# Four x tiles on one DMA queue, the key weights behind ScalarE's table load, and a first stage reordered to match

## The chip, the cores and the metric

The kernel runs on one core of a Trainium2 chip. The metric is the device time of one execution in microseconds (us), the median of several runs of the same program. The core has a matrix engine (TensorE, "PE" in the profile, with its weight loads shown as "PEld"), VectorE ("DVE"), ScalarE ("ACT"), GpSimd ("POOL") and SyncE ("SP"). Each engine runs its own instructions in order; engines meet through semaphores. Loads and stores are issued by an engine into that engine's DMA queue and are carried out by 16 DMA engines that all queues share. In this kernel SP, ACT and POOL issue DMAs.

## The reference

The input `x` has 2048 rows of 512. The block is a linear attention with 32 heads of 16, followed by a gated MLP that mixes the rows; both have a layer norm in front and a residual around them.

```python
# A: linear attention on layernorm(x)
q, k, v = split(x_norm @ wqkv)               # 32 heads of 16
phi = lambda t: where(t > 0, t + 1, exp(t)) + 1e-6
pq, pk = phi(q), phi(k)
kv = einsum('bhsd,bhse->bhde', pk, v)
z  = einsum('bhsd->bhd', pk)
o  = einsum('bhqd,bhde->bhqe', pq, kv) / (einsum('bhqd,bhd->bhq', pq, z) + 1e-6)
h  = x + o @ wo
# B: gated MLP with spatial mixing on layernorm(h)
z1, z2 = split(gelu(h_norm @ w_in)); z2 = layernorm(z2)
g   = einsum('ts,bsf->btf', w_sp, z2) + b_sp
out = h + (z1 * g) @ w_out
```

## The kernel before

The 2048 rows are 16 tiles of 128 rows, called tile 0 to tile 15. The first stage, about the first 41 us, does this for each tile:

- a DMA brings the tile (128 KB) from `A_x`; tiles 0 to 3 come one by one, later ones in pairs, and the last four in one DMA;
- VectorE takes its statistics (`stats`, L576, then `aggr`, L580);
- the reciprocal root is made on ScalarE (L590, L592) for tiles 0 to 3 and on GpSimd (L595, L597) for pairs of later tiles;
- VectorE normalises it (`normalise`, L611);
- it is transposed: tiles 0 to 3 by four TensorE transposes (L645, called T0 to T3 here) and a ScalarE copy out of PSUM (L652); tiles 4 to 15 by a DMA transpose that SP issues (L637);
- TensorE multiplies it with the key weights (`kv_proj`, L734, four matmuls of 128x128x512, called K0 to K15), which need the transposed tile and the weights `wk`;
- ScalarE and VectorE make phi of a pair of tiles (L711, L713, L714, L717, L720);
- TensorE accumulates the product of phi(k) and the normalised x (L766, in units of two matmuls, called X here).

Query projections (`q_proj`, L748, units of four matmuls, called Q) need four transposed tiles and the weights `wq`; they are filled in between. Sums over phi(k) (L782) close the stage. After that come the denominators, the attention output (L904), the two halves of the MLP's first matmul (L936, L967), the row mixing (L1006) and the output projection (L1024).

TensorE also runs matmuls on constants (`keep_busy`, L564): eight when the kernel starts, two after the first statistics, one of 512 columns after the first reciprocal root, and two pairs of 256 columns that are placed behind T0 and T1 in the order written out by hand. They change no result.

The order of every engine is not decided while the kernel is built. `ORDER` lists all operations by number, and each engine issues its own operations in that sequence; `SLOT` gives, for each tile of PSUM and of the scratch buffers in turn, the buffer that it takes. `Program.schedule` turns both into per-engine lists, and `_waits` into semaphore waits: an operation waits for what its data and its buffer need, and everything behind it on its engine waits with it. The costs written beside the operations take no part in what the chip does.

Before the change the first DMAs are issued so: SP issues x tile 0, x tile 2, x tile 3, `wq`, then the x tiles 4-5, 6-7, 8-9, 10-11 and 12-15; ScalarE issues x tile 1 and `wk`, and then loads its function table (L555). GpSimd fills constants: the identity for the transposes (L526, L527), `eps` (L530), masks (L538 to L542) and a selection matrix (L548, L550).

Of the kernel before, what the change touches and what calls it, by code (L numbers as in the profile page):

```python
# [12 lines left out]


ORDER = [
# [34 lines left out]
]  # L50
SLOT = [
# [104 lines left out]
class Program:  # L156
# [14 lines left out]
    def op(self, eng, cost, fn, r=(), w=(), bias=0.0, after=(), dma=None, nbytes=0, land=2.0, lag=None,  # L171
           mode=0):
        o = Op()
        o.eng, o.fn, o.cost, o.seq = eng, fn, cost, len(self.ops)
        o.bias, o.land, lag = bias + self.bias, land, self.LAG[eng] if lag is None else lag
        o.late, o.start, o.mode = self.late, None, mode
        o.after, o.deps, o.tiles = list(after) + self.first_of.get(eng, []), {}, []
        o.marked, o.sem, o.semval, o.grp, o.bytes, o.lag = False, None, None, dma, nbytes, lag
        o.raw = set()
        for x in list(r) + list(w):  # L180
            t = getattr(x, "tile", None)
            if t is not None and t not in o.tiles:
                o.tiles.append(t)
                t.ops.append(o)
        rk = [k for x in r for k in x.keys]
        wk = [k for x in w for k in x.keys]
        for k in rk:
            p = self.writer.get(k)
            if p is not None:
                o.deps[p] = True  # L190
                o.raw.add(p)
        for k in wk:
            p = self.writer.get(k)
            if p is not None:
                o.deps[p] = True
            for q in self.readers.get(k, ()):
                if q is not o:
                    o.deps[q] = True
        for k in rk:
            self.readers.setdefault(k, []).append(o)  # L200
        for k in wk:
            self.writer[k] = o
            self.readers[k] = []
        self.ops.append(o)
        return o
# [149 lines left out]
def bass_sequential_preLN__linear_attn_block__mixer_gmlp__prompt_kernel(  # L355
# [11 lines left out]
    _, S, D = A_x.shape  # L367
# [41 lines left out]
    wqkv = View(s_w3, 0, [KD, 3 * D], BF16)  # L409
# [84 lines left out]
    def load(eng, name, dst, src, nbytes, bias=0.0, behind=(), cost=0.5):  # L494
        o = op(eng, cost, lambda e: e.dma_start(dst.ap(), src), w=[dst], dma=(name, False), nbytes=nbytes,
               bias=bias, land=2.3)
        for p in behind:
            o.deps[p] = True
        return o

    w3 = A_wqkv.rearrange("(c p) f -> p c f", p=P)
# [3 lines left out]
    def load_x(eng, a, b, bias=BIG, **kw):  # L505
        more = {2: 40e3, 3: 60e3, 4: 70e3}.get(a, 0)
        xl[a] = load(eng, f"x{a}", x[a:b, :], x_dram[a * P:b * P, :].rearrange("(n p) d -> p n d", p=P),
                     int((b - a) * P * D * 2 + more), bias, **kw)

    load_x("sp", 0, 1)  # L510
    load_x("act", 1, 2)
    load("act", "wk", wqkv[:, D:2 * D], w3[:, :, D:2 * D], D * D * 2)
    load_x("sp", 2, 3)
    load_x("sp", 3, 4)
    load("sp", "wq", wqkv[:, 0:D], w3[:, :, 0:D], D * D * 2)
# [20 lines left out]
    def blocks(t, n, w, size):  # L536
# [18 lines left out]
    table = op("act", 1.3, lambda e: e.preload_act_table_set("natural_log_exp_and_others"), bias=BIG - 1,  # L555
               after=[o for o in g.ops if o.eng == "act"])
    g.first_of["act"] = [table]

    idle = Tile(PS)
    warm = []  # L560
# [523 lines left out]
```

## Time and profile before

| what | value |
|---|---|
| median of 3 runs | 241.23 us (240.99 to 241.85) |
| profiled execution, its own time | 241.31 us |
| span of that execution, first to last instruction | 240.1 us |
| granted TensorE clock, mean over the span | 1.000 |
| TensorE busy | 235.3 us |
| VectorE, ScalarE, GpSimd busy | 132.8, 78.6, 33.3 us |

The profiled execution takes 1.2 us more than its span: that part lies before the first and after the last instruction. A busy time counts an engine's instructions from start to end. The profile has several views: the page with its totals; the chain of waits that ended last, in order of time; the timeline of instructions; the DMA issues with their time from issue to landing; and a table of busy times by stretches. In the timeline a row has the start, the duration, the engine, the line, what is written and read, how many instructions were merged (`x4`), and in brackets the idle time before it and what ended it. `SPq` and `ACTq` rows are DMA issues: their duration is the issuing engine's time, not the transfer's. The chain counts an operation from the end of the one before it, so its starts can differ from the timeline's by up to 0.2 us.

### The profile page before, as it was taken

The page shows a single profiled execution, that of the slowest core. Times are in us where ns is not written, and L with a number is a line of the kernel's source. Part 1 is how long each engine was busy: PE and PEld are TensorE (multiplying, and loading weights), DVE is VectorE, ACT ScalarE, POOL GpSimd, SP SyncE. Part 2 cuts the span into 40 slices and gives each one's busy share as a digit, 9 for nine tenths or more (in the row PEclk, how much of TensorE's full clock was granted, in tenths as well). Part 3 has the DMA queues.
Part 4 walks back from the last instruction along what each step waited for, and adds up shares of the span by engine and source line. Part 5 has one row for each costly group of instructions (what it writes and reads, how often), then busy time and mean ns, then how long its engine had stood idle before and what let it go on. Part 6 is the DMA issues. An engine that isn't in the chain of part 4 may idle for free.

```text
span 240.1 us, 3026 instructions
## 1 busy us (share of the span) xinstructions
PE 235.3 (98%) x1172; PEld 110.2 (46%) x1194; DVE 132.8 (55%) x269; ACT 78.6 (33%) x101; POOL 33.3 (14%) x84
## 2 busy tenths in 40 slices
PE   7999999999999999999999999999999999999996
PEld 2544444554444444444444444444444444444443
DVE  4898884489999882938533233351332523323444
ACT  3783843884487698665400000000000000000000
POOL 7131303000334514235000000000000000000000
DMA  6930539950214463369444444445500200000022
GB/s 215 310 77 19 105 70 252 322 104 3 44 33 93 122 83 66 67 172 159 108 91 107 90 104 94 109 93 88 148 24 0 67 24 0 0 3 0 0 87 88
DMA packets 56702, 21.83 MB, mean 91 GB/s; under 512 B 50704, under 2 KB 55824, under 8 KB 56688
## 3 DMA queue, kind: packets, MB, share of 16 engines
q1 hardware_dynamic: 54928, 16.62, 33.3%
q0 software_dynamic: 944, 4.33, 5.4%
q10 hardware_dynamic: 816, 0.70, 0.9%
q8 instruction: 9, 0.15, 0.3%
q14 instruction: 5, 0.04, 0.1%
HBM read 7.47 MB, written 2.10 MB: 40 GB/s over the span
## 4 chain that ended last, share of the span: by engine, by line
PE 96%; DMA 1%; DVE 1%; issue 1%
PE ps L1006 40%; PE ps L936 10%; PE ps L1024 10%; PE ps L967 10%; PE ps L766 6%; PE ps L904 6%; PE ps L734 6%; PE ps L748 6%; DMA xh<-in_A_x_dram 1%; DVE small L576 1%; PE ps L645 1%; PE ps L858 0%; PE ps L838 0%; PE ps L782 0%; PE ps L874 0%
## 5 line engine op out<-in xcount | busy, mean ns | idle before, releaser
L1006 PE MATMUL ps<-wsp,pk_xn_z 128*128 128x512 bf16 x328 | 72.9, 379 | 0.4
L1013 DVE TENSOR_TENSOR e<-ps,e 128x512 bf16<-128x512 f32 x28 | 19.4, 692 | 66.1 <-PE ps L1006 66.1
L1006 PEld LDWEIGHTS ps<-wsp,pk_xn_z 128*128 128x128 bf16 x336 | 32.9, 98 | 39.6
L936 PE MATMUL ps<-win,hT 128*128 128x512 bf16 (+1 forms) x127 | 26.1, 352 | 0.1
L967 PE MATMUL ps<-hT,win 128*128 128x512 bf16 x108 | 25.8, 379 | 0.2
L1024 PE MATMUL ps<-wout,xT_pq_z 128*128 128x512 bf16 (+2 forms) x118 | 24.6, 366 | 0.1
L1006 PE MATMUL ps<-wqkv_wsp,pk_xn_z 128*128 128x512 bf16 x110 | 24.2, 379 | 0.1
L945 DVE BATCH_NORM_STATS2 small<-pk_xn_z 128x6 f32<-128x512 bf16 (+1 forms) x32 | 18.2, 606 | 10.6 <-ACT pk_xn_z L941 10.6
L576 DVE BATCH_NORM_STATS2 small<-xh 128x6 f32<-128x512 bf16 x32 | 21.0, 675 | 3.5 <-DMA xh<-in_A_x_dram 3.5
L711 ACT ACTIVATE e<-ps 128x1024 bf16<-128x1024 f32 x16 | 16.4, 1029 | 11.5 <-PE ps L734 8.1
L936 PEld LDWEIGHTS ps<-win,hT 128*128 128x128 bf16 x128 | 12.5, 98 | 12.7
L972 ACT ACTIVATE xT_pq_z<-ps 128x1024 bf16<-128x1024 f32 (+1 forms) x16 | 14.2, 915 | 10.0 <-PE ps L967 10.0
L1024 PEld LDWEIGHTS ps<-wout,xT_pq_z 128*128 128x128 bf16 x119 | 11.5, 98 | 13.0
L1030 DVE TENSOR_TENSOR e<-ps,xh 128x512 bf16<-128x512 f32 (+2 forms) x17 | 11.2, 660 | 11.3 <-PE ps L1024 11.3
L1006 PEld LDWEIGHTS ps<-wqkv_wsp,pk_xn_z 128*128 128x128 bf16 x112 | 11.0, 98 | 13.2
L967 PEld LDWEIGHTS ps<-hT,win 128*128 128x128 bf16 x112 | 10.9, 98 | 12.5 <-DVE xh L909 0.2
L941 ACT ACTIVATE pk_xn_z<-ps 128x896 bf16<-128x896 f32 x16 | 14.5, 918 | 4.6 <-PE ps L936 4.6
L597 POOL TENSOR_TENSOR small<-small 128x2 f32<-128x2 f32 x22 | 15.8, 720 | 1.3
L766 PE MATMUL ps<-pk_xn_z 128*128 128x512 bf16 x64 | 15.9, 379 | 0.0
L734 PE MATMUL ps<-wqkv_wsp,xT_pq_z 128*128 128x512 bf16 x63 | 15.6, 379 | 0.1
L748 PE MATMUL ps<-xT_pq_z,wqkv_wsp 128*128 128x512 bf16 x60 | 14.6, 379 | 0.3 <-issue 0.2
L904 PE MATMUL ps<-pk_xn_z,xT_pq_z 128*128 128x512 bf16 x63 | 14.2, 379 | 0.2 <-issue 0.2
(71 smaller groups left out, 173.0 us busy)
## 6 DMA issues: line engine op xcount, KB each, us to landing
out_dram<-e SPq DMA_DIRECT2D x15, 128.0 KB, 1.7
win<-in_B_w_in_dram POOLq DMA_DIRECT2D x1, 1792.0 KB, 11.3
xh<-in_A_x_dram SPq DMA_DIRECT2D x4, 256.0 KB, 6.2
wout<-in_B_w_out_dram POOLq DMA_DIRECT2D x1, 896.0 KB, 6.8
wsp<-in_B_w_sp_dram SPq DMA_TRANSPOSE x48, 2.7
wqkv_wsp<-in_A_wqkv_dram ACTq DMA_DIRECT2D x1, 512.0 KB, 4.4
wqkv_wsp<-in_A_wqkv_dram SPq DMA_DIRECT2D x1, 512.0 KB, 5.6
xh<-in_A_x_dram SPq DMA_DIRECT2D x1, 512.0 KB, 7.4
```

The lines of the kernel that those rows point to most:

```text
L576: op("dve", dve_c(512), lambda e: e.bn_stats(s6.ap(), src.ap()), r=[src], w=[s6])
L711: op("act", act_c(n), lambda e: e.activation(lo.ap(), t(flat).ap(), ACT.Exp), r=[t()], w=[lo])
L734: i = e.matmul(t(bank(ti)).ap(), lhsT=lhs.ap()[:, c, :], rhs=rhs.ap()[:, c, :], start=(c == 0), stop=(c == KD - 1))
L748: r_ = e.matmul(t(bank(i)).ap(), lhsT=lhs.ap()[:, c, :], rhs=rhs.ap()[:, c, :], start=(c == 0), stop=(c == KD - 1))
L766: r = e.matmul(txk[h](bank(i)).ap(), lhsT=xx.ap()[:, c * P:(c + 1) * P], rhs=kk.ap(), start=(n == 0), stop=(n == NT - 1))
L904: i = e.matmul(t(bank(ti)).ap(), lhsT=l.ap()[:, c, :], rhs=mw[c, :].ap(), start=(c == 0), stop=(c == KD - 1))
L936: k = e.matmul(t(bank(i)).ap()[:, 0:b - a], lhsT=l.ap()[:, c, :], rhs=win[c, a:b].ap(), start=(c == 0), stop=(c == KD - 1))
L945: op("dve", dve_c(b - a), lambda e, s6=s6, src=src: e.bn_stats(s6.ap(), src.ap()), r=[src], w=[s6])
L967: k = e.matmul(t(bank(i)).ap(), lhsT=l.ap()[:, c, :], rhs=r_.ap()[:, c, :], start=(c == 0), stop=(c == KD - 1))
L1006: k = e.matmul(t(bank(0)).ap(), lhsT=l.ap()[:, s - a, :], rhs=r_.ap()[:, s - a, :], start=(s == 0), stop=(s == NT - 1))
L1013: op("dve", dve_c(512), lambda e: e.tensor_tensor(gb().ap(), t(bank(0)).ap(), bsp().ap()[:, tg * GW:(tg + 1) * GW], ALU.add), r=[t(), bsp( ...
L1024: k = e.matmul(t(bank(0)).ap()[:, 0:b - a], lhsT=l.ap()[:, fc, :], rhs=wout[fc, a:b].ap(), start=(fc == 0), stop=(fc == KF - 1))
```

## The change

The change has three parts.

First, x tile 1 is issued by SP as the second of its DMAs, so tiles 0 to 3 come from one queue in order, and each later DMA on SP is one place further back. ScalarE issues no x tile.

Second, `wk` is still issued by ScalarE, but behind the table load and not ahead of it.

Third, `ORDER` and `SLOT` are replaced for the first stage. Read out of the two lists, and with F for a filling matmul of 512 columns and f for one of 256, the orders at the start are:

```
TensorE  before  T0 F f f T2 K0 T1 K2 f T3 f K1 K3 Q Q Q Q  X X X K4 K5 X X X K6 X X X X K7 Q Q X X Q Q K8 K9
TensorE  after   T0 F f f T1 f f K0 T2 K1 T3 K2 K3 Q Q Q Q  X X X K4 K5 X X K6 X X X X X K7 X Q X Q K8 K9
VectorE  before  stats 0, 2, norm 0, stats 1, norm 2, stats 3, norm 1, norm 3, stats 5, 4, ...
VectorE  after   stats 0, 1, norm 0, stats 2, norm 1, stats 3, norm 2, norm 3, stats 4, 5, ...
ScalarE  before  x tile 1, wk, table, root 0, root 2, copy 0, root 1, copy 2, root 3, copy 1, copy 3, phi ...
ScalarE  after   table, wk, root 0, root 1, copy 0, root 2, copy 1, root 3, copy 2, copy 3, phi ...
GpSimd   before  L530 L548 L531 L532 L538 L533 L526 L527 L539 L538 L550 L542 L539 L542 L534
GpSimd   after   L532 L533 L538 L530 L538 L539 L548 L526 L531 L550 L527 L539 L542 L542 L534
```

Ahead of the normalising of tile 8, VectorE before also had the statistics of tile 13 and the first phi step of a query pair; after, these come behind it, and the aggregate of tile 12 comes ahead. The second query pair of rows 512 to 1023 moves from ahead of K8 to behind K15. No instruction is added or taken away on any engine except that the issue of x tile 1 goes from ScalarE to SP. From L782 on, the orders are the same as before.

```diff
 ORDER = [
-    0, 3, 4, 5, 6, 27, 1, 2, 13, 24, 14, 28, 29, 30, 31, 32, 33, 15, 21, 16, 7, 8, 34, 35, 123, 124, 11, 12, 22, 18,
-    25, 23, 19, 36, 20, 49, 50, 9, 10, 26, 37, 38, 39, 51, 52, 40, 42, 17, 125, 126, 53, 127, 41, 43, 56, 54, 44, 130,
...
+    0, 1, 2, 3, 4, 5, 14, 6, 7, 8, 9, 15, 20, 12, 17, 18, 25, 26, 23, 10, 13, 24, 27, 28, 29, 30, 31, 32, 11, 35, 36,
+    42, 43, 37, 38, 33, 34, 123, 21, 22, 39, 124, 44, 45, 19, 49, 40, 46, 41, 125, 126, 127, 47, 128, 129, 50, 56, 51,
...
 SLOT = [
-    0, 1, 1, 2, 1, 4, 0, 4, 0, 2, 1, 2, 1, 6, 1, 2, 0, 6, 0, 2, 2, 6, 0, 6, 0, 2, 6, 0, 6, 6, 2, 6, 2, 0, 6, 1, 6, 6,
...
+    0, 1, 2, 2, 2, 4, 0, 2, 4, 0, 1, 0, 1, 6, 1, 6, 1, 0, 1, 6, 1, 0, 2, 6, 2, 2, 6, 0, 6, 6, 0, 6, 0, 2, 6, 1, 6, 6,
...
     load_x("sp", 0, 1)
-    load_x("act", 1, 2)
-    load("act", "wk", wqkv[:, D:2 * D], w3[:, :, D:2 * D], D * D * 2)
+    load_x("sp", 1, 2)
     load_x("sp", 2, 3)
     load_x("sp", 3, 4)
     load("sp", "wq", wqkv[:, 0:D], w3[:, :, 0:D], D * D * 2)
...
     table = op("act", 1.3, lambda e: e.preload_act_table_set("natural_log_exp_and_others"), bias=BIG - 1,
                after=[o for o in g.ops if o.eng == "act"])
     g.first_of["act"] = [table]
+    load("act", "wk", wqkv[:, D:2 * D], w3[:, :, D:2 * D], D * D * 2)
```

20 rows, old and new, of tables (ORDER, SLOT) are left out of this document.

## The prediction, made before the changed kernel was run

> **What bounds the kernel now.** I read the page's totals first, then the chain of waits, then the timeline of the first 45 us, then the DMA issues of each short stretch. The page's first part:
>
> ```profile
> PE 235.3 (98%) x1172; PEld 110.2 (46%) x1194; DVE 132.8 (55%) x269; ACT 78.6 (33%) x101; POOL 33.3 (14%) x84
> ```
>
> TensorE is busy for 235.3 of 240.1 us, and the change adds and removes no matmul. So the time can move only by when TensorE's useful work begins and by the holes after that. The table of busy times gives the holes of the stage that the change touches:
>
> ```profile
> core 0: us, PE busy (x) PEld busy (x) DVE busy (x) ACT busy (x) POOL busy (x), PEclk, DMA share, GB/s
> 5.76:11.17 5.41, 5.41 (x37) 3.03 (x38) 4.57 (x13) 3.72 (x10) 0.63 (x2) 1.00 1.09 352
> 11.17:41.00 29.83, 29.67 (x136) 13.90 (x137) 24.11 (x55) 18.41 (x20) 7.75 (x14) 1.00 0.43 95
> ```
>
> From 11.17 to 41 us TensorE lacks 29.83 - 29.67 = 0.16 us: a new order has nothing to win there, and much to lose. The DMA share of 1.09 says that the DMA engines are full in the first stretch, at 352 GB/s. The chain of waits shows what comes ahead of TensorE:
>
> ```profile
> 0.79 2.68 DMA xh<-in_A_x_dram
> 3.50 0.70 DVE small L576
> 4.23 0.18 DVE small L580
> ...
> 5.76 0.58 PE ps L645 x4
> ...
> 9.17 0.11 PE ps L564
> 9.28 0.22 PE ps L645 x4
> ...
> 9.61 1.73 PE ps L734 x8
> ```
>
> x tile 0 lands at 0.79 + 2.68 = 3.47, its statistics follow at once, and T0, the first useful work, starts at 5.76. After that the chain is TensorE alone. Three unit costs come from here: f takes 0.11 us, a T 0.22, a K 1.73 / 2 = 0.86. A Q is four matmuls of the same shape, 0.86, and an X two, 0.43.
>
> **The landings.** The change moves the place or the time of nearly every load. These are rows of the timeline (the one at 1.70 from a shorter stretch, where it stands alone), and below them the landings, each from a query of a stretch of the DMA issues that holds that DMA alone of its kind (in this order: x tile 2 issued by SP at 1.25, x tile 3 at 1.70, `wk` at 1.23, `wq` at 2.17, x tiles 4-5 at 2.65):
>
> ```profile
> 0.79 0.40 ACTq L495 DMA_DIRECT2D xh<-in_A_x_dram  x1
> 0.79 1.33 SPq L495 DMA_DIRECT2D xh<-in_A_x_dram  x3
> 1.23 0.46 ACTq L495 DMA_DIRECT2D wqkv_wsp<-in_A_wqkv_dram  x1
> 1.70 0.42 SPq L495 DMA_DIRECT2D xh<-in_A_x_dram  x1
> 1.71 1.28 ACT L555 ACT_TABLE_LOAD   x1 [1.71 <-PEq L1069]
> 2.17 0.43 SPq L495 DMA_DIRECT2D wqkv_wsp<-in_A_wqkv_dram  x1
> 2.65 2.61 SPq L495 DMA_DIRECT2D xh<-in_A_x_dram  x5
> ```
>
> ```profile
> xh<-in_A_x_dram SPq DMA_DIRECT2D x1, 128.0 KB, 2.9
> ...
> xh<-in_A_x_dram SPq DMA_DIRECT2D x1, 128.0 KB, 4.3
> ...
> wqkv_wsp<-in_A_wqkv_dram ACTq DMA_DIRECT2D x1, 512.0 KB, 4.4
> ...
> wqkv_wsp<-in_A_wqkv_dram SPq DMA_DIRECT2D x1, 512.0 KB, 5.6
> ...
> xh<-in_A_x_dram SPq DMA_DIRECT2D x1, 256.0 KB, 5.8
> ```
>
> An issue takes SP about 0.45 us. So after the change x tiles 1, 2, 3 go out at 1.25, 1.70 and 2.17, `wq` at 2.65, and every later load one place, some 0.46 us, later. On ScalarE the table load starts at 0.79 instead of 1.71 and ends at 2.07; `wk` goes out there, 0.84 us later than now. What reads each of them, and when:
>
> ```profile
> 4.33 0.66 DVE L576 BATCH_NORM_STATS2 small<-xh 128x6 f32<-128x512 bf16 x1
> ...
> 5.54 0.67 DVE L576 BATCH_NORM_STATS2 small<-xh 128x6 f32<-128x512 bf16 x1
> ...
> 6.54 0.66 DVE L576 BATCH_NORM_STATS2 small<-xh 128x6 f32<-128x512 bf16 x1
> ...
> 7.44 0.41 DVE L611 TENSOR_SCALAR pk_xn_z<-xh,small 128x512 bf16<-128x512 bf16 x1 [0.24 <-ACT small L592]
> ...
> 8.54 0.41 DVE L611 TENSOR_SCALAR pk_xn_z<-xh,small 128x512 bf16<-128x512 bf16 x1 [0.60 <-ACT small L592]
> ```
>
> VectorE comes to the second, third and fourth tile at 4.33, 5.54 and 6.54, whichever they are; VectorE and ScalarE keep the same pattern with tiles 1 and 2 exchanged.
> - x tile 0: nothing is issued ahead of it, and x tile 1 no longer travels beside it. It can gain between nothing and 0.3 us. The 0.3 is an estimate: x tile 2, issued 0.46 us behind it with one more load on the way, took 2.9, so a companion costs about 0.2, and I add half as much for the unknown. A loss has no cause, as it stays the first. I take 0.1, nearer to nothing, since the 2.7 and the 2.9 differ so little.
> - x tile 1: 1.25 + 2.9 = 4.15, from its present neighbour in the same place of the queue; needed at 4.33. Bounds 2.7 to 4.3: at 4.3 it lands at 5.55 and T0, whose normalising stands behind these statistics, is 1.2 us late. I take 2.9, since what made x tile 3 take 4.3, `wk` issued ahead of it, is now issued behind.
> - x tiles 2 and 3: 2.9 gives 4.6 and 5.1, 4.3 gives 6.0 and 6.5; needed at 5.54 and 6.54. The first is hidden. If x tile 2 falls behind `wk` as x tile 3 does now, its 0.46 us of lateness passes to T2, but only 0.34 of it shows (T2 has 0.12 of cover, below).
> - `wk`: 2.07 + 4.4 = 6.5, with bounds 2.9 and 5.6, so 5.0 to 7.7. Needed when K0 can start.
> - `wq` is needed at about 11 and lands near 8. x tiles 4-5 keep the same bytes ahead of them; with full DMA engines the landing, 2.65 + 5.8 = 8.45 now, moves by at most the 0.46 of the issue, to 8.91. VectorE comes to them when the fourth normalising ends, at 8.95: hidden.
> - GpSimd's identity, needed by T0, now comes behind the long selection fill. The row below ends at 4.29; of what stands ahead of it, two short fills leave and one comes. The identity is ready by about 4.6, T0 starts at 5.76: hidden, with 1.1 us of cover.
>
> ```profile
> 2.70 1.59 POOL L550 TENSOR_SCALAR_AFFINE_SELECT wsp<-wsp 128x512 bf16<-128x512 bf16 x1
> ```
>
> **TensorE up to the first Q.**
>
> ```profile
> 6.67 0.38 PE L645 MATMUL ps<-small,pk_xn_z 128*128 128x128 bf16 x4
> ...
> 7.04 0.55 PEld L734 LDWEIGHTS ps<-wqkv_wsp,xT_pq_z 128*128 128x128 bf16 x4 [0.16 <-ACT xT_pq_z L652]
> ...
> 11.17 1.03 PE L748 MATMUL ps<-xT_pq_z,wqkv_wsp 128*128 128x512 bf16 x3
> ```
>
> Now the second transpose starts at 6.67 and ends at 6.89; TensorE then stands for 0.16 us until ScalarE's copy of T0 lets K0 start at 7.04. Both f that now stand further back (0.22 us) move into that hole. After the change: T1 to 6.89, two f to 7.11, K0 to 7.97, T2 to 8.19, K1 to 9.06, T3 to 9.28, K2 and K3 to 11.01 (rounded sums), where the first Q starts, against 11.17: 0.15 us won. Their inputs: T2 needs the third normalising, 7.44 + 0.41 = 7.85, 0.12 us ahead; T3 the fourth, 8.95, 0.11 us ahead. The cover is thin: what x tile 2 or x0's chain loses beyond 0.12 us shows in full. K3 waits for the copy of T3, which now ends just as it did; I count 0 to 0.05 lost there.
>
> **From the first Q to K8.** Now 12 units of 0.86 and 12 of 0.43 lie between the first Q and K8: 15.5 us, and 11.17 + 15.54 = 26.71 is when K8 runs.
>
> ```profile
> 21.32 0.40 DVE L714 TENSOR_SCALAR e<-e 128x1024 bf16<-128x1024 bf16 x1
> ...
> 21.63 0.69 DVE L576 BATCH_NORM_STATS2 small<-xh 128x6 f32<-128x512 bf16 x1
> ...
> 22.23 0.72 DVE L611 TENSOR_SCALAR pk_xn_z<-xh,small 128x512 bf16<-128x512 bf16 x2
> ...
> 26.71 1.89 PE L734 MATMUL ps<-wqkv_wsp,xT_pq_z 128*128 128x512 bf16 x8
> ```
>
> ```profile
> 22.66 1.19 SPq L637 DMA_TRANSPOSE xT_pq_z<-pk_xn_z  x1
> ```
>
> ```profile
> xT_pq_z<-pk_xn_z SPq DMA_TRANSPOSE x1, 3.1
> ```
>
> Tile 8 is normalised from 22.23, its DMA transpose goes out at 22.66 and lands 3.1 later at 25.75: 0.96 us ahead of K8. After the change two Q are gone from ahead of K8, which comes 1.73 us sooner, and VectorE has a phi step and a statistics less ahead of tile 8 and one aggregate more: by starts 0.31 + 0.60 (21.32 to 21.63 to 22.23), and with what follows in the queue between 0.73 (the aggregate's 0.18 taken off) and 0.91. So the spare falls from 0.96 to between -0.04 and 0.14 us. K9's transpose goes out right behind. I count 0 to 0.3 lost here and take 0.05. This place alone turns from safe to tight. K15 and the last Q pair change places as well; the sums at L782 then wait for that pair's phi to free PSUM; from the 0.16 us of all holes now, I count 0 to 0.15 and take 0.05.
>
> **The sum.** 241.31 - 0.1 (x tile 0) - 0.15 (f in the hole) + 0.05 (K8) + 0.05 (L782) + 0.02 (K3) = 241.18. The profiled execution is 0.08 above the median of the three runs, so the median should be 241.1. With each term at its bounds, -0.3 to 0 for x tile 0 and up to 0.5 lost in the rest, the case runs from 240.8 to 241.7.
>
> A rule that speaks against any gain: the row of SP shows that an issue costs 0.45 us of its engine, which x tile 1 now pays on SP. The Trainium skill (DMA: Bandwidth & Descriptors, "Issuing engines are not separate DMA queues") says that all queues end on the same 16 engines and that issuing from several saves only this issue time. By it x tile 0 gains nothing, and the sum would be 241.2.
>
> **The rivals.** *`wk` arrives too late* (the slower side). While `wk` is carried now, SP has x tile 3 and `wq` waiting. In the stretch from 3.70 to 4.75 the DMA queues show:
>
> ```profile
> q10 hardware_dynamic: 359, 0.37, 100.2%
> q1 hardware_dynamic: 5, 0.00, 1.1%
> ```
>
> ScalarE's queue (q10) gets everything, though SP's two requests are only 0.5 and 0.9 us younger. So the older request seems to go first, and `wk`, issued at 2.07 against 2.65 for `wq`, should still precede it. If instead the two share, `wk` ends with `wq`, at the 2.17 + 5.6 = 7.77 of now. The point is 7.11, when K0 can start: every us behind it counts in full, because all of TensorE is queued behind K0. Price 0.66, time 241.8; if x tiles 4-5 go ahead too, 8.45, price 1.3, time 242.5. The Trainium skill (same page, "Queues, rings and completion order") states that each DMA engine takes the queues in turns, packet by packet; by it this rival is what happens. The trace disagrees: 359 packets against 5.
>
> *The transposes are too slow for K8*. Tile 8's normalising may gain nothing, if VectorE still waits there for something the reorder doesn't move. Then 25.75 stands against 24.83: price 0.9, time 242.1. Against it: the VectorE rows at 21.32, 21.63 and 22.23 have no bracket of idle time, so what leaves ahead of tile 8 is work and not waiting.
>
> *Nothing reaches the end*: x tile 0 lands as now, the won 0.15 is lost at K8 and L782. Time 241.3; it lies inside the forecast's own range.
>
> *x tile 0 gains more*: 0.3 and no loss behind, 240.7.
>
> **The numbers.** Forecast (with the nothing case) 0.70; `wk` with `wq` 0.09, with tiles 4-5 also 0.04; K8 late 0.08; x tile 0 early 0.09. The smallest change that a measurement of this kernel can tell is 0.5%, 1.2 us: below 240.0 or above 242.4. Faster than that needs two gains at their bounds and a lucky median: 0.04. Slower needs `wk` behind tiles 4-5, or K8 and `wk` together: 0.10. Same: 0.86. The range 240.4 to 242.2 leaves out these tails; the likeliest case alone has 240.8 to 241.7.
>
> **What would show it.** Right: T0 at 5.6 to 5.8; no wait of PEld L734 for longer than 0.1 us before the first Q; the first Q at 10.9 to 11.1; `wk` landing before 7.0; K8 near 24.8 with no wait worth 0.3 us; a TensorE busy time of 235.3 as now. Wrong: PEld L734 released by a DMA of `wqkv_wsp` near 7.5 to 8.5; the second statistics waiting for a DMA of `xh`; K8 waiting for a DMA transpose; or an L782 row that waits for ScalarE.

## The result: slower by 1.0%

The changed kernel takes 244.04 us (median of 6 runs, 242.37 to 245.19) against 241.14 us for the kernel before. The ratio of the means of the runs, 243.74 and 241.24, is 1.0104, with a 95% interval of 1.0061 to 1.0146. The profiled execution takes 243.88 us with a span of 242.7 us, 2.6 us more than before. The runs scatter far more than the 241.0 to 241.9 of the kernel before; a part of the reason is shown below.

The first and fourth part of the page, and the table of busy times over the same stretches as before:

```profile
PE 236.2 (97%) x1172; PEld 110.7 (46%) x1194; DVE 132.4 (55%) x269; ACT 78.9 (33%) x101; POOL 32.9 (14%) x84
...
PE 96%; DMA 2%; issue 1%; DVE 1%; SPq 0%
```

```profile
core 0: us, PE busy (x) PEld busy (x) DVE busy (x) ACT busy (x) POOL busy (x), PEclk, DMA share, GB/s
5.76:11.17 5.41, 4.17 (x23) 2.39 (x24) 4.75 (x13) 2.65 (x9) 0.00 (x0) 0.68 1.08 351
...
11.17:41.00 29.83, 29.67 (x140) 13.94 (x142) 22.45 (x55) 18.30 (x20) 8.03 (x15) 1.00 0.40 87
```

From 11.17 to 41 us the holes are the 0.16 us of before. From 5.76 to 11.17 TensorE is busy for 4.17 us instead of 5.41, and its granted clock is 0.68 instead of 1.00. So two things went wrong ahead of 11.17 us, and no hole was added from there to 41 us. The chain of waits of the changed kernel:

```profile
0.80 0.39 SPq L495
1.18 0.06 issue
1.24 4.38 DMA xh<-in_A_x_dram
5.62 0.02 issue
5.65 0.70 DVE small L576
...
7.00 0.38 PE ps L645 x4
...
8.86 1.71 PE ps L734 x4
...
12.15 1.73 PE ps L734 x8
13.88 0.43 PE ps L748 x2
```

The chain no longer begins with x tile 0 but with x tile 1, issued at 1.24 and landing 4.38 us later, at 5.62. T0 starts at 7.00 instead of 5.76, and K0's four matmuls take 1.71 us, where four take 0.86 in the kernel before. One of the prediction's own signs of being wrong is there: the second statistics wait for a DMA of `xh`, for 1.49 us. The timeline says why x tile 1 is late, and the DMA issues, x tile 0 and then x tile 1 each alone in its stretch, agree:

```profile
0.79 1.28 ACT L554 ACT_TABLE_LOAD   x1 [0.79 <-PEq L1069]
...
0.82 0.45 ACTq L495 DMA_DIRECT2D wqkv_wsp<-in_A_wqkv_dram  x1
...
5.65 0.69 DVE L576 BATCH_NORM_STATS2 small<-xh 128x6 f32<-128x512 bf16 x1 [1.49 <-DMA xh<-in_A_x_dram]
...
7.00 0.38 PE L645 MATMUL ps<-small,pk_xn_z 128*128 128x128 bf16 x4 [2.21 <-DVE pk_xn_z L611]
```

```profile
xh<-in_A_x_dram SPq DMA_DIRECT2D x1, 128.0 KB, 2.4
...
xh<-in_A_x_dram SPq DMA_DIRECT2D x1, 128.0 KB, 4.4
```

`wk` stands behind the table load in ScalarE's program but does not wait for it: its issue starts 0.03 us after the load starts and 1.25 us before the load ends. The change moved `wk` not from 1.23 to 2.07 but from 1.23 to 0.82, ahead of x tile 1. In the stretch from 3.2 to 4.25 us, while x tiles 1 to 3 wait, the DMA queues show:

```profile
q10 hardware_dynamic: 281, 0.29, 94.3%
q1 hardware_dynamic: 1, 0.00, 0.3%
```

### The profile page after: what moved, and what is told of

It reads as the page before. It is cut to its first block, busy times and chain, and to the rows that moved or that the text cites. A ratio compares the mean times of both kernels' runs of the same rounds, so it can differ in the third digit from the quotient of the medians.

```text
span 242.7 us, 3027 instructions
## 1 busy us (share of the span) xinstructions
PE 236.2 (97%) x1172; PEld 110.7 (46%) x1194; DVE 132.4 (55%) x269; ACT 78.9 (33%) x101; POOL 32.9 (14%) x84
## 4 chain that ended last, share of the span: by engine, by line
PE 96%; DMA 2%; issue 1%; DVE 1%; SPq 0%
PE ps L1006 40%; PE ps L936 10%; PE ps L1024 10%; PE ps L967 10%; PE ps L734 6%; PE ps L904 6%; PE ps L766 6%; PE ps L748 6%; DMA xh<-in_A_x_dram 2%; PE ps L645 1%; PE ps L858 0%; PE ps L782 0%; PE ps L838 0%; PE ps L564 0%; PE ps L874 0%
## 5 line engine op out<-in xcount | busy, mean ns | idle before, releaser
L734 PE MATMUL ps<-wqkv_wsp,xT_pq_z 128*128 128x512 bf16 x64 | 16.6, 397 | 0.0
```

What stands on the lines that cost most here:

```text
L734: i = e.matmul(t(bank(ti)).ap(), lhsT=lhs.ap()[:, c, :], rhs=rhs.ap()[:, c, :], start=(c == 0), stop=(c == KD - 1))
```

## The experiments

Every run below is timed beside the kernel before on the same chip. Theory 1: a load waits for those issued before it, on either queue, so `wk` at 0.82 us delayed x tile 1. Rival 2: x tile 1 is late because it is second on SP's queue. Rival 3: the new orders cost by themselves. The second term, the clock, has experiments of its own (e0 and e5). The table gathers what was measured; landings are issue plus time to landing in the profiled execution, T0 and the first Q are starts in its chain of waits (in e7, e8 and e9, whose chain lacks T0, from the timeline).

| kernel | `wk` out | x tile 1, 2, 3 in | `wk` in | T0 | first Q | median us | ratio to before, 95% interval |
|---|---|---|---|---|---|---|---|
| before | 1.23 | 3.7, 4.2, 6.0 | 5.7 | 5.76 | 11.33 | 241.14 | |
| changed | 0.82 | 5.6, 6.0, 6.3 | 5.2 | 7.00 | 13.88 | 244.04 | 1.0104 (1.0061 to 1.0146) |
| e0, changed again | 0.83 | 5.6, 6.0, 6.3 | 5.2 | 6.97 | 12.32 | 243.46 | 1.0082 (1.0056 to 1.0109) |
| e5, changed, more fills | 0.82 | 5.7, 6.0, 6.4 | 5.3 | 7.06 | 12.41 | 242.36 | 1.0048 (1.0031 to 1.0065) |
| e4, loads only | 0.82 | 5.6, 6.0, 6.4 | 5.2 | 7.37 | 14.19 | 244.20 | 1.0133 (1.0108 to 1.0157) |
| e3, orders only | 1.25 | 3.5, 3.9, 6.5 | 6.2 | 5.63 | 10.97 | 240.96 | 0.9995 (0.9986 to 1.0005) |
| e6, before, `wk` behind table | 1.25 | 3.8, 4.1, 6.0 | 5.6 | 5.73 | 11.19 | 241.11 | 0.9999 (0.9986 to 1.0012) |
| e7, `wk` held to 1.62 | 1.65 | 3.4, 6.1, 7.0 | 6.6 | 5.24 | 11.66 | 241.53 | 1.0023 (1.0005 to 1.0041) |
| e9, e7 with norm 1 first | 1.65 | 3.4, 6.2, 6.8 | 6.4 | 5.25 | 11.49 | 241.77 | 1.0025 (1.0015 to 1.0035) |
| e8, `wk` held to 1.76 | 1.80 | 3.4, 5.5, 6.6 | 7.1 | 5.10 | 11.28 | 241.31 | 1.0001 (0.9986 to 1.0016) |
| e2, `wk` held to 2.08 | 2.12 | 3.4, 4.4, 5.6 | 6.9 | 5.26 | 11.08 | 241.07 | 0.9992 (0.9980 to 1.0004) |
| e1, `wk` on SP behind x tile 3 | 2.64 | 3.4, 4.0, 4.4 | 7.5 | 5.25 | 11.73 | 241.50 | 1.0012 (1.0001 to 1.0023) |

**e2: the issue time that the prediction assumed.** The changed kernel; only `wk` waits for a GpSimd fill.

```diff
-    op("pool", 0.45, lambda e: e.memset(sel.all().ap(), 0.0), w=[sel.all()], bias=BIG)
+    hold = op("pool", 0.45, lambda e: e.memset(sel.all().ap(), 0.0), w=[sel.all()], bias=BIG)
...
-    load("act", "wk", wqkv[:, D:2 * D], w3[:, :, D:2 * D], D * D * 2)
+    load("act", "wk", wqkv[:, D:2 * D], w3[:, :, D:2 * D], D * D * 2, behind=[hold])
```

In `ORDER`, `wk` (26) goes behind the fill (23).

> The changed kernel, with wk's issue on ScalarE held by a wait for GpSimd's fill of the selection matrix, which ends at 2.08 us: this makes the issue time that the prediction assumed (2.1 instead of the 0.82 that the trace shows). Theory 1: x tile 1 lands at 3.9 to 4.2, wk at 6.0 to 6.6, no wait for it at K0, first Q near 10.9, time 240.8 to 241.2. Rival 2: x tile 1 after 5.4, time 242.4 or more. Rival 3: x tile 1 early and the time above 242.

Measured: x tile 1 lands at 3.4, x tile 2 at 4.4, and the loss is gone: 241.07. Its timeline:

```profile
0.79 1.28 ACT L554 ACT_TABLE_LOAD   x1 [0.79 <-PEq L1069]
...
2.12 0.48 ACTq L495 DMA_DIRECT2D wqkv_wsp<-in_A_wqkv_dram  x1
...
2.96 0.69 DVE L576 BATCH_NORM_STATS2 small<-xh 128x6 f32<-128x512 bf16 x1 [2.96 <-DMA xh<-in_A_x_dram]
...
7.02 1.02 PE L734 MATMUL ps<-wqkv_wsp,xT_pq_z 128*128 128x512 bf16 x4 [0.24 <-ACT small L592]
```

One issue time was changed, and x tile 1 comes 2.2 us sooner from the same place of the same queue. Rivals 2 and 3 fall. One of e2's eleven runs took 245.68 us with a mean clock of 0.993; it is not in the ratio and was not traced. A point of theory 1's expectation missed: `wk` lands at 6.9, not by 6.6, and K0 waits 0.24 us. The row names a ScalarE instruction (L592, done at 6.88) that K0 does not need. By the waits that the kernel writes, K0 needs two things, the copy of T0 on ScalarE, done at 6.47, and `wk`, in at 6.89; so `wk` ended the wait.

**e1: nothing ahead of the x tiles.** `wk` on SP between x tile 3 and `wq`.

```diff
-    load("act", "wk", wqkv[:, D:2 * D], w3[:, :, D:2 * D], D * D * 2)
+    load("sp", "wk", wqkv[:, D:2 * D], w3[:, :, D:2 * D], D * D * 2)
```

> The changed kernel, with wk issued by SP behind x tile 3 and ahead of wq, so that nothing is issued ahead of x tiles 1 to 3. Theory 1 (loads are served in the order of their issue, over both queues, and wk at 0.82 us passed x tile 1): x tile 1 lands at 3.9 to 4.2 instead of 5.62, T0 starts at 5.4 to 5.8, wk lands at 6.3 to 7.0 and holds K0 by 0.2 at most, the clock stays at 1.0, and the time is 240.8 to 241.2. Rival 2 (x tile 1 is late because it is second on SP's queue): it lands after 5.4 all the same and the time is 242.4 or more. Rival 3 (the new orders cost by themselves): landings as in theory 1, but the time stays above 242.

Measured: the x tiles land at 3.0, 3.4, 4.0 and 4.4, 2.2 to 2.3 us behind their issues and sooner than theory 1 said (3.9 to 4.2 for x tile 1), so rival 2 falls again. The time misses theory 1's number: `wk`, issued at 2.64, takes 4.8 us and lands at 7.5, and the chain has K0 at

```profile
7.60 1.02 PE ps L734 x4
```

This edit brings about the prediction's own slower rival: behind the point of 7.11 the wait for `wk` shows.

**e3 and e4: the two halves of the change.** e3 keeps the new orders and issues x tile 1 on ScalarE again, ahead of the table load; e4 keeps the old orders with the new issues.

```diff
 e3, against the changed kernel
-    load_x("sp", 1, 2)
+    load_x("act", 1, 2)
 e4, against the kernel before: the changed kernel's four load lines, ORDER renumbered for them
```

> The changed kernel's orders with x tile 1 issued by ScalarE again, ahead of the table load and of wk, so that the loads go out as before the change. Theory 1: landings within 0.2 us of those of before, wk out near 1.25, time 241.0 to 241.3, TensorE without a wait over 0.3 us at K8. Rival 3 (the orders cost): 242 or more with the same landings.

> The orders of before with the changed issues alone (x tiles 0 to 3 by SP, wk by ScalarE behind the table load). The second tile to be used is then x tile 2. Theory 1: x tile 1 lands at 5.6 and x tile 2 at 6.0, T0 starts near 7.4 and not at 5.8, and the time is 242.7 if the clock stays up and 244.3 if it falls to half for the first matmuls. Rival 3: 241.1, since the old orders are in place.

Measured: e3 240.96, not told apart from before. Its landings are not all within the 0.2 us that I expected: x tile 3 and `wk` come 0.5 later than before (6.5 and 6.2). Its first Q starts at 10.97, 0.36 sooner than before; of that, 0.13 is T0. Its K8 runs, in the timeline, at

```profile
24.62 1.89 PE L734 MATMUL ps<-wqkv_wsp,xT_pq_z 128*128 128x512 bf16 x8
```

without a wait. So the orders cost nothing that these runs show, and K8's thin spare held. e4 loses 1.3%: the loads alone make the loss, and rival 3 falls.

**e6: the table load by itself.** The kernel before, with `wk` put behind the table load and nothing else moved.

> The kernel before, with wk behind the table load and nothing else moved: x tile 1 stays on ScalarE. If a table load doesn't hold back ScalarE's DMA issues, wk goes out at 1.2 to 1.3 us as before and nothing changes: 241.0 to 241.3. If it does, wk goes out at 2.1 or later, lands near 6.9, and K0 waits for less than 0.2 us: 241.1 to 241.4, with x tile 3 landing earlier than its 6.0. The issue time and the landing of x tile 3 tell these apart, the time hardly.

Measured: 241.11, no difference. Its timeline shows the load and the issue side by side:

```profile
1.22 1.28 ACT L549 ACT_TABLE_LOAD   x1 [1.22 <-PEq L1064]
1.25 0.43 ACTq L490 DMA_DIRECT2D wqkv_wsp<-in_A_wqkv_dram  x1
```

**e7, e8 and e9: `wk` between the x tiles.** e7 holds `wk` by the first selection on a GpSimd mask (ended at 1.62), e8 by the identity's first fill, put ahead of the other fill. e9 is e7 with one exchange in `ORDER` (49, the statistics of tile 2, behind 46, the normalising of tile 1).

> The changed kernel with wk's issue held until GpSimd's first selection on a mask ends, at 1.62 us, between the issues of x tile 1 (1.24) and x tile 2 (1.70). Theory 1 (service in order of issue): x tile 1 lands at 3.4 to 3.7 as with the longer hold, wk at 5.8 to 6.4, x tiles 2 and 3 later than with the longer hold (4.4 to 6.2); K0 near 6.8, time 240.7 to 241.0, the lowest of all. If what counts is a fixed share between queues and not the order, x tile 1 comes later by about a third of the way to the 5.6 of the changed kernel, at 4.1 or more, and the time is 241.2 or more.

> The changed kernel with the identity's first fill moved ahead of the selection matrix's on GpSimd, and wk's issue held until that fill ends, at about 1.76 us: behind the issue of x tile 2 (1.70) and ahead of that of x tile 3 (2.17). Service in order of issue: x tile 2 lands at 3.9 to 4.5 again (6.05 with the hold that ends at 1.62), x tile 3 at 5.6 to 6.2, which is hidden, and wk 0.3 us earlier than the 6.89 of the longer hold; K0 at 6.6 to 6.9 instead of 7.02, time 240.7 to 241.0, below both kernels. If x tile 2 is passed by wk even so, because its issue takes SP until 2.12, it lands near 6 and the time is 241.4 to 241.6, as with the shorter hold.

> The kernel with wk held until 1.62 us (241.53 us, x tile 2 landing at 6.05), with one exchange on VectorE: the normalising of tile 1 goes ahead of the statistics of tile 2. If its loss against the longer hold comes from T1, whose normalising stands behind the statistics of the late x tile 2, T1 starts at 6.0 to 6.3 and not at 7.1, K0 at 6.7 to 6.9 (wk lands near 6.6), the first Q at 10.8 to 11.1 and not at 11.66, and the time is 240.8 to 241.1. If the late tile costs elsewhere too (its own transpose T2), the time stays at 241.3 or more.

Measured: in e7 `wk` goes out 0.05 us before x tile 2, and now x tile 2 is the late one, at 6.1, while x tile 1 is in at 3.4. The order of issue decides which tile is hit here, and a fixed share between the queues doesn't fit. My time for e7 (240.7 to 241.0) was wrong: VectorE has the statistics of tile 2 ahead of the normalising of tile 1, so T1 waits. In e8 `wk` goes out 0.10 us behind x tile 2, whose issue holds SP until 2.12; x tile 2 lands at 5.5 and `wk` at 7.1. That is the second branch of its expectation but for the size. So the rule of order is not sharp where two issues overlap. A tile issued first by 0.10 takes 3.8 us (x tile 2, e8), one issued second by 0.05 takes 3.5 (x tile 3, e2) or 4.4 (x tile 2, e7), and x tile 0 of the changed kernel, first by 0.03, takes 2.4. What decides there is not shown. e9 says where the late x tile 2 costs: K0 starts at 6.57 in its timeline, a little sooner than I expected, but TensorE waits 0.71 us for T2:

```profile
8.30 0.38 PE L647 MATMUL ps<-small,pk_xn_z 128*128 128x128 bf16 x4 [0.71 <-DVE small L582]
```

So the time stays up, at 241.77, which is the second branch of e9's expectation (241.3 or more).

**e0 and e5: the clock.** e0 is the changed kernel again. e5 is the changed kernel with three matmuls in each of the two fills behind the first statistics.

```diff
-            keep_busy(n, cost, [], [gate] if gate.eng != "pe" else [])
+            keep_busy(n, cost, [], [gate] if gate.eng != "pe" else [],
+                      3 if gate is first[0] else 1)
```

> The changed kernel once more, as the base of this call. Theory 1 with the clock as a second term: its runs fall at two places, near 242.4 where the clock stays up through the wait for x tile 1, and near 244.0 where TensorE runs at half clock for some 3 us behind that wait. Theory 1 without that term: all runs near 242.4 to 243.

> The changed kernel, with each of the two filling matmuls behind the first statistics made three, so that TensorE stands idle for 0.5 us and not for 2.2 us ahead of T0; the loads are not touched, and x tile 1 still lands at 5.6. If half of the loss is the clock that falls while TensorE waits, the clock is 1.0 in every stretch, T0 starts at 7.0 as in the changed kernel, the first Q at 12.3 to 12.6 instead of 13.7, and the time is 242.2 to 242.6 in every run. If the clock plays no part (the late landing costs 2.5 us by its wait alone), it stays at 243.8 or more.

Measured: e0's six runs are 242.22, 242.33, 243.44, 243.48, 243.83 and 243.88 (median 243.46). e5's eight runs all lie between 242.26 and 242.58. The busy times per microsecond in the changed kernel:

```profile
7.00:8.00 1.00, 1.00 (x9) 0.59 (x10) 1.00 (x4) 0.70 (x3) 0.00 (x0) 0.80 1.11 363
8.00:9.00 1.00, 1.00 (x7) 0.69 (x6) 0.95 (x3) 0.93 (x4) 0.00 (x0) 0.50 1.10 349
9.00:10.00 1.00, 1.00 (x4) 0.36 (x3) 0.43 (x2) 0.51 (x3) 0.00 (x0) 0.50 1.11 349
10.00:11.00 1.00, 1.00 (x7) 0.67 (x6) 1.00 (x2) 0.00 (x0) 0.00 (x0) 0.50 1.10 349
11.00:12.00 1.00, 1.00 (x9) 0.51 (x8) 0.97 (x4) 0.60 (x1) 0.43 (x2) 0.99 0.59 187
```

And the same stretch, 5.76 to 11.17, in the profiled executions of e0 (242.33 us) and then of e5 (242.41 us):

```profile
5.76:11.17 5.41, 4.19 (x33) 2.33 (x33) 4.75 (x13) 3.60 (x11) 0.00 (x0) 1.00 1.10 351
```

```profile
5.76:11.17 5.41, 4.10 (x33) 2.33 (x33) 4.75 (x13) 3.51 (x10) 0.00 (x0) 1.00 1.08 350
```

In the changed kernel's profiled execution the clock is at half for 0.4 + 3 + 0.02 = 3.4 us. The 0.80 of the first row puts its start near 7.6, some 0.6 us behind the start of T0 and not in the wait. In e0's it stays at 1.00 though x tile 1 lands at 5.6 there too. The chain of e0 has T0 and the first Q at

```profile
6.97 0.38 PE ps L645 x4
...
12.32 0.43 PE ps L748 x2
```

5.35 us apart, against 13.88 - 7.00 = 6.88 in the changed kernel's: 1.53 us of clock, and the times of the two executions differ by 243.88 - 242.33 = 1.55. e5's mean clock is 1.000 in every run, and the wait for x tile 1 is left. TensorE still stood for about 1.5 us ahead of T0 in e5, not the 0.5 that I had planned, since the four added matmuls made the fills only 0.29 us longer (4.71 against 4.42 in e0's timeline); the expected time held all the same. The Trainium skill (TensorE: Matmul & The Clock Gate, "Part 1: The HAM clock gate") says that the clock is judged over free-running windows of about 3.4 us, so that the same program meets them at a different phase from run to run. The trace agrees in this: half clock for 3.4 us, in some executions of one program and not in others.

How long TensorE must stand for it, these runs do not show. The clock fell where TensorE stood for 2.21 us ahead of T0 (changed) and 2.57 us (e4), and stayed up after 1.72 us (e0) and 1.52 us (e5). In the first two the ten filling matmuls ahead of T0 also ended sooner, at 4.79 against e0's 5.25, so the length of the wait and the phase are not told apart. A late x tile 1 may not be the only thing that brings it: one run of e2 (245.68) and one of e7 (243.47) have the mean clock of 0.993 too, and in the profiled executions of both x tile 1 is in at 3.4. What makes the runs near 243.45, whose mean clock is reported as 1.000, and the one of 245.19, was not traced and stays open.

## Why the prediction was wrong

**Where 2.57 us came from** (243.88 against 241.31, the profiled executions): T0 is 7.00 - 5.76 = 1.24 late; from T0 to the first Q the half clock adds 1.53; and the new order takes 5.57 - 5.35 = 0.22 off the way from T0 to the first Q. The sum is 2.55. From the first Q to the end of the span the two take the same: 240.1 - 11.33 = 228.8 and 242.7 - 13.88 = 228.8.

**The step that failed** is the sentence "On ScalarE the table load starts at 0.79 instead of 1.71 and ends at 2.07; `wk` goes out there". Nothing quoted shows that a table load holds back a DMA issue; I took the order of the program for an order in time. The runs show the issue 0.03 us behind the start of the load: at 0.82 in the changed kernel, and at 1.25 behind a load at 1.22 in e6. So `wk` went out ahead of x tile 1, which took 4.38 us and not 2.9. The later step, that x tile 1 takes 2.9 "since what made x tile 3 take 4.3, `wk` issued ahead of it, is now issued behind", fell with it. The upper bound that I had written for x tile 1 came true to the number: "at 4.3 it lands at 5.55 and T0 [...] is 1.2 us late"; measured 4.38, 5.62 and 1.24. The bound stood in the text and got no rival and no chance, and my range ended before it.

e2 makes the issue time that I assumed, and its 241.07 is the 241.1 of the forecast. That is in part luck: x tile 0 won 0.5 us and not 0.1, and the wait of K0 for `wk`, which I had at nothing, took it back.

**The term that was missing** is the clock. I priced a late T0 at its wait alone. With 1.5 us for half clock added, that bound would have given 241.18 + 1.2 + 1.5 = 243.9. Of the twelve runs of the changed kernel (e0's among them), five lie at 243.83 to 244.20 and four, near the bound without the clock, at 242.22 to 242.58.

**Right, by the runs.** The two f in K0's hole: 0.15 predicted, 0.22 measured from T0 to the first Q (e0). K8 without a wait: predicted at 24.83 with a spare of -0.04 to 0.14, found at 24.62 in e3 without one. Nothing added at L782, which starts at 41.0 in the kernel before and at 43.6 in the changed one: from the first Q to the end both take 228.8. Service by order of issue and not by turns: 281 packets against 1 now, as 359 against 5 before, which again is not what the Trainium skill (DMA: Bandwidth & Descriptors, "Queues, rings and completion order") says of turns between queues; only the overlapping issues of e8 and e2, 0.10 and 0.05 us apart, come out in between. And `wk` too late beyond about 7.1: e1 at 7.60.

**Wrong in size.** x tile 0's gain: I took 0.1 of at most 0.3; alone on the way it lands after 2.1 to 2.2 us (e1, e2), some 0.5 sooner than before. It is not won: e2's T0 starts 0.5 sooner, and K0 at 7.02, as before. The prediction had `wk` in at 6.5, ahead of the 7.11 at which K0 was to be ready; with T0 at 5.26 and `wk` in at 6.9, `wk` comes last.

No version was found that is clearly below both: e3 and e2 are the lowest, and their intervals hold 1.

## What to carry to other kernels

Read the issue time of a DMA from the issue row, and not from its place behind a long instruction of the same engine: the table load did not move it (e6), a wait on a semaphore did (e2). A large load that goes out a fraction of a microsecond before a small one that everything waits for can make the small one land behind it (2.2 us later for x tile 1 here), so give the first-needed loads the first issues and keep the bulk behind them by a wait if need be, but not so far that it becomes late itself (e1). When TensorE may wait near its start, price the wait and the clock behind it (1.5 us here, where it stood for 2.2 us), and put filling matmuls where the wait may be (e5).

## What was not expected of the hardware

- ScalarE issues a DMA during its own table load: 0.03 us behind the start of the 1.28 us load, in every kernel here that has this order without a wait (changed, e3, e4, e6).
- x tiles with no large load ahead of them land 2.2 to 2.3 us behind their issue for four in a row (e1), against 4.2 to 4.4 with 512 KB issued ahead of them.
- The granted clock's column reads 1.00 while the first matmuls run at half rate. In e2's chain of waits, ten matmuls of 512 columns ahead of T0 take 0.44 us each, twice the 0.22 of later ones, and the table of busy times has 1.00 for the same stretch. So a mean clock of 1.000 does not show that a run was at full rate from its start:

```profile
0.83 4.43 PE ps L564 x10
```

```profile
0.83:5.28 4.45, 4.45 (x11) 1.34 (x12) 2.25 (x6) 2.24 (x5) 4.31 (x15) 1.00 0.71 178
```
